# Attention and mixer on one core: where score steps stand between matmuls, and how the last output tile is stored

## The chip, the core and the metric

One NeuronCore of a Trainium2 chip runs the whole program. Its engines are TensorE (PE, matmuls; PEld is its weight load), VectorE (DVE), ScalarE (ACT), GpSimd (POOL) and SyncE (SP), which here only issues DMAs. Each engine executes its own queue in order; semaphores hold an instruction until what it reads is there and what it overwrites has been read. The metric is the time of one execution in microseconds on the device, the median of several runs.

## The reference

Eight items of 448 tokens, 12 heads of 64. Attention with normalised queries and keys, then a mixer on the result: a low-rank product over tokens, and a two-layer MLP.

```python
q_n, k_n = rmsnorm(q, g_q), rmsnorm(k, g_k)
attn = softmax(q_n @ k_n^T / sqrt(64))            # per item and head, 448 x 448
x = (attn @ v) as [8, 448, 768]                   # heads side by side
u = x + (x^T @ U @ V)^T                           # U: 448 x 32, V: 32 x 448
out = u + max(u @ w_ch1, 0) @ w_ch2               # 768 -> 3072 -> 768
```

## The kernel before

Work comes in two kinds, kept in two lists that are written out when the kernel is built. `att` holds attention steps, `mlp` holds mixer steps. A loop at the end takes from one or the other and so fixes the order of every engine's queue.

Attention goes by groups of four heads (24 groups, three an item; group 18, say, is heads 0 to 3 of item 6) and, inside, by pairs of heads (two a group, six an item). `load` brings q, k and v of a group; `squares` (ACT or POOL) and `sums` (VectorE, one reduction for q, one for k, L162) give the sums of squares; `scale_all` takes the roots on ACT (L169, L170) and scales q, k and v on POOL (L193 to L203). From group 6 on, `turn_dma` transposes q and k by DMA (issued by SP, L378 and L380) and `take_dma` multiplies the transposed queries by the gains on POOL (L386).

`Spair(b, pr)` computes all scores of one pair of heads: two matmuls into two banks `sl` (L427), four into `sc` (L436), one into a third bank `sl` (L438); ACT then takes five exponentials (L429, L439, L441). `V(b, pr, half)` is the product with the values (L462, L466), divided by the row sums on VectorE (L469, L470).

The mixer of item b: `mix_t(b)` (L485) is x^T U, cast by VectorE to `tb` (L487); `mix_tr(b)` (L492) transposes it, VectorE copies it to `tT` (L494); eight `mix_rows(b, w, half)` (L537) multiply with V and add to x on VectorE (L542), and after each second one SP issues the DMA transpose of u into `uT` (L548). 24 steps `up(b, ht)` (L554, six matmuls of 448 columns) make the hidden layer, with ReLU on ACT into `hT` (L561). `down(b, col, half, part, 4)` (L586) makes half an output tile of 128 tokens in four parts of six matmuls of 384 columns; behind the last part VectorE adds u (L596), and after the second half SP stores the tile, 64 x 768 numbers twice (L604).

Eight PSUM banks: four belong to `sc` (two tiles of two banks), four to the pool `ps`, from which `sl`, `pv`, `pu`, `pw`, `pm`, `ph` and `po` all come. Each new tile is given the bank of an earlier one, so its first matmul waits until whoever read that earlier tile last is done.

`due(c)` says how much attention (`ca`) should be placed when `c` of the mixer's cost is placed. An attention step is taken when it is due and `ready`. `at` holds, for PE, ACT and DVE, an estimated time up to which that engine has work, moved by `runs`; before the change `ready` looks at it only in the first part (`ca < a_one`), and refuses a `Spair` straight behind a mixing step. `mix_t`, `mix_tr` and `mix_rows` of the next item stand among the `down` steps of the current one; where one comes up right behind a `Spair`, a `down` part is drawn ahead of it (`after_pair`).

Of the kernel before, what the change touches and what calls it, by code (L numbers as in the profile page):

```python
# [9 lines left out]
FP32 = mybir.dt.float32  # L10
# [3 lines left out]
ALU = AluOpType  # L14
# [5 lines left out]
DMA_FROM = 6  # L20
# [6 lines left out]
def kernel(  # L27
# [13 lines left out]
    nc = tc.nc  # L41
    B, H, S, D = q.shape
    dm = H * D
# [3 lines left out]
    P = 128  # L47
    NT = S // 64
    NJ = S // P
    SM = NJ * P  # L50
    R = S - SM
# [6 lines left out]
    KH = dh // P  # L58
    NPAIR = H // 2
    HALF = dm // 2  # L60
# [9 lines left out]
    outp = ctx.enter_context(tc.tile_pool(name="outp", bufs=3))  # L70
    ps_sc = ctx.enter_context(tc.tile_pool(name="ps_sc", bufs=2, space=bass.MemoryType.PSUM))
    ps = ctx.enter_context(tc.tile_pool(name="ps", bufs=4, space=bass.MemoryType.PSUM))
# [199 lines left out]
    w2b = consts.tile([P, KH, dm], BF16)  # L272
    hT = consts.tile([P, KH, 512], BF16)
# [63 lines left out]
    at = {"pe": 0.0, "act": 0.0, "dve": 0.0}  # L337
    exp_done = {}

    def runs(eng, us):  # L340
        at[eng] = us + (at["pe"] if eng == "pe" else max(at["pe"], at[eng]))

    qk, es, xs = {}, {}, {}
# [136 lines left out]
    def mix_t(b):  # L480

        pt = ps.tile([P, KD, rank], FP32, name="pu", tag="ps")
        for dt in range(KD):
            for j in range(NW):
                nc.tensor.matmul(pt[:, dt, :], xs[b][:, j, dt * P:(dt + 1) * P], Ub[:, j if j < NJ else NJ + b % 2, :],  # L485
                                 start=(j == 0), stop=(j == NW - 1))
        nc.vector.tensor_copy(tb_bufs[b % 2][:, :KD * rank], pt.rearrange("p k r -> p (k r)"))  # L487

    def mix_tr(b):
        pt = ps.tile([P, 2, P], BF16, name="pw", tag="ps")  # L490
        for i in range(2):
            nc.tensor.transpose(pt[:, i, :], tb_bufs[b % 2][:, i * P:(i + 1) * P], ident)  # L492
        tTs[b] = headp.tile([P, 2, P], BF16, name="tT", tag="tT")
        nc.vector.tensor_copy(tTs[b], pt)  # L494

    def mix_t0(lo, hi, scalar=False):

        pt = ps.tile([P, 512], FP32, name="pu0", tag="ps")
        for j in range(NW):
            nc.tensor.matmul(pt[:, :hi - lo], Uz[:, j, :], xs[0][:, j, lo:hi], start=(j == 0), stop=(j == NW - 1))  # L500
        if scalar:
            nc.scalar.copy(tz[:, lo:hi], pt[:, :hi - lo])
        else:
            nc.vector.tensor_copy(tz[:, lo:hi], pt[:, :hi - lo])
# [70 lines left out]
            nc.scalar.activation(hT[:, ht, off:off + S], ph, AF.Relu)  # L575

    down_ps, down_sb = {}, {}

    def down(b, col, half, part, nparts):
        key = (b, col, half)  # L580
        if part == 0:
            down_ps[key] = ps.tile([P, HALF], FP32, name="po", tag="ps")
        po = down_ps[key]
        n = KH // nparts
        for ht in range(part * n, (part + 1) * n):
            nc.tensor.matmul(po, hT[:, ht, col:col + P], w2b[:, ht, half * HALF:(half + 1) * HALF],  # L586
                             start=(ht == 0), stop=(ht == KH - 1))
        runs("pe", 0.98)
        if part < nparts - 1:
            return  # L590
        runs("dve", 0.55)
        h = slice(half * HALF, (half + 1) * HALF)
        if half == 0 or b == 0:
            down_sb[(b, col)] = outp.tile([P, dm], FP32, name="ob", tag="ob")
        ob = down_sb[(b, col)]
        nc.vector.tensor_tensor(ob[:, h], po, urows(b, col, half), ALU.add)  # L596
        if half == 1 or b == 0:
            h = h if b == 0 else slice(0, dm)

            def rows(b, j):  # L600
                return out[b].rearrange("(p j) d -> j p d", j=NT)[j]
            for i in range(2):
                o = rows(b, i * NJ + col // P) if col != SM else rows(b - i, 2 * NJ)
                nc.sync.dma_start(o[:, h], ob[i * R:(i + 1) * R, h])  # L604
# [10 lines left out]
    def weights(n):  # L615
        for f, a in todo[:n]:
            f(*a)
        del todo[:n]
# [51 lines left out]
    for i, (b, pr) in enumerate(pairs):  # L670
        if b == 0:
            continue
        gi, a = divmod(i, 2)
# [78 lines left out]
    mlp = []  # L752
    for b in range(B):
        for ht in range(KH):
            mlp.append((0.38, up_part, (b, ht, 4, KD), b) if b == 0 and ht < 2 else (1.14, up, (b, ht), b))
            if b < ROWS_FROM and ht % 2 == 0 and ht < 4 * NW:
                mlp.append((0.17, mix_rows, (b, ht // 4, ht // 2 % 2), b))
        cols = (64, 192, 320) if b % 2 == 0 else (384, 0, 128, 256)
        n = len(cols) * 8
        nb = b + 1  # L760
        pre = {}
        if ROWS_FROM <= nb < B:
            pre[n - PRE[nb > 1]] = [(0.77, mix_t, (nb,), nb)]
            pre[n - PRE[nb > 1] + 1] = [(0.11, mix_tr, (nb,), nb)]
            for piece in range(2 * NW):
                pre.setdefault(n - PRE[nb > 1] + 2 + (piece if nb > 1 else piece // 2), []).append(
                    (0.17, mix_rows, (nb, *divmod(piece, 2)), nb))
        tiles = [(col, half) for col in cols for half in range(2)]
        if b == 0:
            tiles.sort(key=lambda t: t[1])  # L770
        for c, (col, half) in enumerate(tiles):
            for part in range(4):
                mlp.extend(pre.get(c * 4 + part, []))
                mlp.append((0.98, down, (b, col, half, part, 4), b))

    a_, b_ = PARTS
    squares_part(0, *a_)
# [40 lines left out]
    ca = cm = 0.0  # L818
    a_from = done_at[0]
    a_all = sum(c for c, _, _ in att[a_from:])  # L820
    a_one = sum(c for c, _, _ in att[a_from:done_at[1]])
# [9 lines left out]
    def due(c):  # L831

        if c < m_one:
            return min(a_one - 0.01, a_one * c / (m_one - 3.0))
        c -= m_one
        if c < REST:
            return a_one - 0.01
        if c < SECOND:
            return a_one + (a_two - a_one) * (c - REST) / (SECOND - REST)
        return a_two + (a_all - a_two) * (c - SECOND) / (m_end - m_one - SECOND)  # L840

    def mixes(f):
        return f in (mix_t, mix_tr, mix_rows)

    def ready(f, a):
        if f is Spair:
            return im == 0 or not mixes(mlp[im - 1][1])
        if ca >= a_one:
            return True
        if f is V:  # L850
            return exp_done[a[:2]] <= at["pe"] + 0.1
        return f is not Srows or at["act"] <= at["pe"] + 0.6

    later, turning, after_pair = [], False, False
    while ia < len(att) or im < len(mlp):
        if not turning:
            for f, a in later:
                f(*a)
            later.clear()
        if ia == a_from and im == 0:  # L860
            at.update(pe=0.0, act=0.0, dve=0.0)
        may_mlp = im < len(mlp) and ia >= done_at[mlp[im][3]]
        take_att = ia < len(att) and (not may_mlp or ca <= due(cm) and ready(*att[ia][1:]))
        if take_att:
            c, f, a = att[ia]
            if f is load:
                later.append((f, a))
            else:
                f(*a)
            after_pair = f is Spair or after_pair and f is not V  # L870
            if ia >= a_from:
                ca += c
            ia += 1
            if f is scale_all and a[0] < DMA_FROM:
                weights(2)
            if f is T and a == (DMA_FROM - 1, 1):
                nc.vector.memset(kp[:, 2 * NJ:], 0.0)
        else:
            if after_pair and mixes(mlp[im][1]):
                nb, n, moved = mlp[im][3], im, []  # L880
                while mixes(mlp[n][1]) and mlp[n][3] == nb:
                    e = next(i for i in range(n, len(mlp)) if mlp[i][1] is down)
                    moved += [mlp[e], *mlp[n:e]]
                    n = e + 1
                mlp[im:n] = moved
            after_pair = False
            c, f, a, _ = mlp[im]
            f(*a)
            turning = f is mix_t and a[0] > 0 or turning and a != (a[0], NW - 1, 1)
            cm += c  # L890
            im += 1
# [30 lines left out]
```

## Time and profile before

| | |
|---|---|
| median of 3 runs | 586.94 us (586.19 to 587.28) |
| the profiled execution, its own time | 586.64 us |
| its span in the profile | 584.8 us |
| granted TensorE clock | 0.999 |
| TensorE, busy share of the span | 98% |
| VectorE, ScalarE, GpSimd | 34%, 53%, 36% |

A row of the timeline reads: start in us, length in us, engine, line, operation, output<-inputs, shape, count, and in brackets the idle time before it with what ended it. A row of a group reads: busy time, mean ns of one, idle time before and what ended it. Rows of the chain of waits have start, length and what was waited for. Matmuls are pipelined: the next starts before the last one's modelled end, so lengths of PE rows overlap.

### The profile page before, as it was taken

Reading aid. Unit: us, or ns where it says so; the run is one execution under the profiler, and the core shown is the slowest. Engines: PE = TensorE matmul, PEld = TensorE weight load, DVE = VectorE, ACT = ScalarE, POOL = GpSimd, SP = SyncE. Lnnn points to the kernel's source line nnn. Section 1 sums busy time; section 2 is a strip of 40 time slices with the busy share of each in tenths; the row PEclk is TensorE's granted clock in tenths of the full one; section 3 lists DMA queues with packets and bytes.
Section 4 is the critical chain, followed back from the end, with each engine's and each line's share of the span. In section 5 each row is a group of like instructions: output and inputs, shape, how many; then the busy total and the mean of one; then the engine's idle time right before and its main releaser. Section 6 shows DMA issues by size and latency. Waiting matters only on the chain.

```text
span 584.8 us, 11725 instructions
## 1 busy us (share of the span) xinstructions
PE 572.2 (98%) x4826; PEld 338.2 (58%) x4826; DVE 196.8 (34%) x458; ACT 307.9 (53%) x510; POOL 210.3 (36%) x310
## 2 busy tenths in 40 slices
PE   8899999999999999999999999999999999999996
PEld 7555556555665555655556555665556655655563
DVE  6676656212352232521235231442034310410011
ACT  7866661677445776277653578457753344014200
POOL 5995684265314515334523433441531000000000
PEclk9999999999999999999999999999999999999999
DMA  8899999683546642585246735375204210420022
GB/s 229 170 241 241 244 233 231 119 220 52 133 78 167 153 106 35 139 212 130 36 122 109 180 104 123 66 172 149 35 25 92 48 28 1 68 61 1 1 54 55
DMA packets 104509, 68.21 MB, mean 117 GB/s; under 512 B 66568, under 2 KB 101256, under 8 KB 104456
## 3 DMA queue, kind: packets, MB, share of 16 engines
q1 hardware_dynamic: 95044, 58.03, 42.6%
q0 software_dynamic: 9408, 9.44, 9.6%
q8 instruction: 38, 0.62, 0.4%
q14 instruction: 15, 0.12, 0.1%
q10 hardware_dynamic: 4, 0.00, 0.0%
HBM read 52.20 MB, written 11.01 MB: 108 GB/s over the span
## 4 chain that ended last, share of the span: by engine, by line
PE 91%; DMA 3%; DVE 2%; POOL 1%; ACT 1%; issue 1%; SPq 1%; POOLq 0%; ACTq 0%
PE ph L554 36%; PE po L586 36%; PE pv L466 6%; PE sc L436 2%; PE sl L427 2%; PE sl L438 2%; PE pv L462 2%; PE pm L537 2%; DMA qf<-in_q_dram 1%; PE sc L415 1%; ACT E L416 1%; DMA vf<-in_v_dram 1%; DVE ssq L162 1%; DMA qT<-qn 1%; PE pu L485 1%
## 5 line engine op out<-in xcount | busy, mean ns | idle before, releaser
L586 PE MATMUL po<-w2b,hT 128*128 128x384 bf16 x1344 | 237.4, 326 | 0.0
L554 PE MATMUL ph<-uT,w1b 128*128 128x448 bf16 x1140 | 228.7, 352 | 0.0
L586 PEld LDWEIGHTS <-hT 128*128 128x128 bf16 x1344 | 126.8, 98 | 75.5 <-issue 0.6
L554 PEld LDWEIGHTS <-w1b 128*128 128x128 bf16 x1140 | 108.3, 98 | 93.8 <-issue 0.7
L561 ACT ACTIVATE hT<-ph 128x448 bf16<-128x448 f32 x184 | 98.0, 550 | 120.2 <-PE ph L554 118.9
L429 ACT ACTIVATE E<-sl,gg 128x448 bf16<-128x448 f32 x72 | 41.5, 629 | 75.9 <-PE sl L427 75.9
L386 POOL TENSOR_SCALAR qT<-qT,gg 128x448 bf16<-128x448 bf16 x36 | 50.5, 1402 | 81.6 <-DMA qT<-qn 65.2
L193 POOL TENSOR_TENSOR qn<-qf,rs 128x384 bf16<-128x384 f32 x36 | 29.9, 829 | 132.4 <-ACT rs L170 127.5
L469 DVE RECIPROCAL r<-pv 128x4 f32<-128x4 f32 x96 | 17.4, 182 | 167.8 <-PE pv L466 167.6
L441 ACT ACTIVATE E<-sc,gg 128x896 bf16<-128x896 f32 x72 | 69.0, 1022 | 0.0
L596 DVE TENSOR_TENSOR ob<-po,x 128x384 f32<-128x384 f32 x48 | 26.7, 557 | 103.8 <-PE po L586 103.4
L466 PE MATMUL pv<-va,E 128*128 128x65 bf16 x1152 | 57.1, 194 | 0.0
L466 PEld LDWEIGHTS <-E 128*128 128x128 bf16 x1152 | 50.5, 98 | 6.3
L162 DVE TENSOR_REDUCE ssq<-sq 128x14 f32<-128x896 f32 x45 | 46.8, 1078 | 2.4 <-ACT sq L140 2.3
L462 PE MATMUL pv<-vl,E 128*128 128x130 bf16 x192 | 42.2, 220 | 0.3 <-ACT E L416 0.2
L470 DVE TENSOR_TENSOR x<-pv,r 128x256 bf16<-128x256 f32 x96 | 40.7, 424 | 3.3
L416 ACT ACTIVATE E<-sc,gg 128x896 bf16<-128x896 f32 (+1 forms) x42 | 37.5, 950 | 4.1 <-PE sc L415 4.1
L542 DVE TENSOR_TENSOR x<-pm,x 128x384 bf16<-128x384 f32 x48 | 26.2, 552 | 16.5 <-PE pm L537 14.2
L193 POOL TENSOR_TENSOR kp<-kf,rs 128x384 bf16<-128x384 f32 x36 | 29.8, 828 | 0.0
L169 ACT ACTIVATE rs<-ssq,eps 128x28 f32<-128x28 f32 (+1 forms) x25 | 7.8, 314 | 33.4 <-DVE ssq L162 29.2
L462 PEld LDWEIGHTS <-E 128*128 128x128 bf16 x192 | 18.7, 97 | 9.7 <-issue 2.0
L439 ACT ACTIVATE E<-sl,gg 128x448 bf16<-128x448 f32 x36 | 22.9, 637 | 0.0
(102 smaller groups left out, 387.9 us busy)
## 6 DMA issues: line engine op xcount, KB each, us to landing
qf<-in_q_dram SPq DMA_DIRECT2D x23, 448.0 KB, 3.7
kf<-in_k_dram SPq DMA_DIRECT2D x23, 448.0 KB, 6.4
out_dram<-ob SPq DMA_DIRECT2D x50, 192.0 KB, 2.8
vf<-in_v_dram SPq DMA_DIRECT2D x48, 192.0 KB, 5.9
w1b<-in_moe_w_ch_dram POOLq DMA_DIRECT2D x4, 1152.0 KB, 19.8
w2b<-in_moe_w_ch_dram POOLq DMA_DIRECT2D x8, 576.0 KB, 17.7
vf<-in_v_dram SPq DMA_DIRECT2D x48, 32.0 KB, 5.7
out_dram<-ob SPq DMA_DIRECT2D x12, 96.0 KB, 3.6
```

The lines of the kernel that those rows point to most:

```text
L162: nc.vector.tensor_reduce(ssqs[gi][:, i, :], sqs.pop((gi, i)), AX, ALU.add)
L193: nc.gpsimd.tensor_tensor(main.rearrange("p (t i) d -> p i t d", i=2), src[:, c, :2 * NJ].rearrange("p (i t) d -> p i t d", i=2), rs[:, c, ...
L386: nc.gpsimd.tensor_scalar(qT[:, a], qT[:, a], gg[:, 0:1], None, ALU.mult)
L416: nc.scalar.activation(es[(b, pr)][:, 2 * r:2 * r + n, :], sc[:, :n, :S], AF.Exp, scale=scal, bias=bias)
L429: nc.scalar.activation(E[:, 4 + i, :], ts[i], AF.Exp, scale=scal, bias=bias)
L441: nc.scalar.activation(E[:, 2 * r:2 * r + 2, :], tiles[r][:, :, :S], AF.Exp, scale=scal, bias=bias)
L462: nc.tensor.matmul(pv[:, i].rearrange("p e d -> p (e d)"), E[:, 2 * NJ, w:w + P], vl[:, lp, :], start=True, stop=False)
L466: nc.tensor.matmul(pv[:, i, e, :], E[:, 2 * j + e, w:w + P], va[:, (first_h + step * e) * NJ + j, :], start=False, stop=(e == 1 and j == N ...
L470: nc.vector.tensor_tensor(xs[b].rearrange("p i (h d) -> p i h d", d=D)[:, 2 * half:2 * half + 2, h0:h0 + step + 1:step, :], pv[:, :, :, :D ...
L554: nc.tensor.matmul(ph, w1b[:, dt, ht * P:(ht + 1) * P], uT[:, dt, off:off + S], start=(dt == 0), stop=(dt == KD - 1))
L561: nc.scalar.activation(hT[:, ht, off:off + S], ph, AF.Relu)
L586: nc.tensor.matmul(po, hT[:, ht, col:col + P], w2b[:, ht, half * HALF:(half + 1) * HALF], start=(ht == 0), stop=(ht == KH - 1))
```

## The change

Three things.

1. The steps `mix_t` and `mix_tr` now move the estimates in `at`.
2. `ready` has new rules for all of the run: a `Spair` is taken only if VectorE's estimate is at most 0.3 us and ACT's at most 1.0 us past PE's; a `V` waits for one mixer step if a `Spair` or another `V` has been taken since the last one; `sums` of groups past 6 aren't taken within a few mixer steps of `mix_t` and `mix_tr`.
3. The last output tile (item 7, token columns from 256) is no longer two halves of four parts. `down_end` makes it in three accumulations of 384, 256 and 128 columns, 24 matmuls each; each is added and stored alone, 64 rows by SP and 64 rows by ACT's queue.

In the program that results, everything up to `down(0, 64, 1, 3)` stands as before. Behind it these steps stand elsewhere; all else keeps its order.

- Spair (2,0), (2,1), (5,4), (6,3), (7,2), (7,4), (7,5): behind one more `down` part; for (6,3) and (7,4) also behind one more `mix_rows`.
- Spair (2,2): behind `up(1, 3)`.
- Spair (3,2): behind three more `down` parts and `mix_rows(2, 3, 1)`.
- Spair (4,2): behind two more `down` parts and `mix_rows(3, 3, 0)` and `(3, 3, 1)`.
- Item 4's mixing: `mix_t(4)` and `mix_tr(4)` come before sums(17) and scale_all(17); Spair (5,2) five `down` parts later, behind `mix_tr(4)` and four `mix_rows(4)`; V(5, 1, 0) and V(5, 1, 1) behind it, turn_dma(17) with it.
- Item 5's mixing: the same for `mix_t(5)`, `mix_tr(5)`, sums(20), scale_all(20), Spair (6,2), V(6, 1), turn_dma(20).

On SP, the transposes of groups 17 and 20 stand one `uT` transpose later than before; on ACT one `hT` comes ahead of the exponentials of Spair (2,2), and the three stores of the last tile stand at the end.

```diff
         nc.vector.tensor_copy(tb_bufs[b % 2][:, :KD * rank], pt.rearrange("p k r -> p (k r)"))
+        runs("pe", 0.62)
+        runs("dve", 0.35)
...
         nc.vector.tensor_copy(tTs[b], pt)
+        runs("pe", 0.11)
+        runs("dve", 0.3)
...
+    ENDS = (HALF, 5 * P, dm)
+
+    def down_end(b, col, piece):
+        lo, hi = (0, HALF) if piece == 0 else ENDS[piece - 1:piece + 1]
+        if piece == 0:
+            down_sb[(b, col)] = outp.tile([P, dm], FP32, name="ob", tag="ob")
+        ob = down_sb[(b, col)]
+        po = ps.tile([P, HALF], FP32, name="po", tag="ps")[:, :hi - lo]
+        for ht in range(KH):
+            nc.tensor.matmul(po, hT[:, ht, col:col + P], w2b[:, ht, lo:hi], start=(ht == 0), stop=(ht == KH - 1))
+        nc.vector.tensor_tensor(ob[:, lo:hi], po, xs[b][:, col // P, lo:hi], ALU.add)
+        for i, eng in enumerate((nc.sync, nc.scalar)):
+            eng.dma_start(out[b].rearrange("(p j) d -> j p d", j=NT)[i * NJ + col // P][:, lo:hi],
+                          ob[i * R:(i + 1) * R, lo:hi])
...
+        if b == B - 1:
+            tiles = tiles[:-2]
...
+    mlp.extend((3.9 * w, down_end, (B - 1, cols[-1], piece), B - 1) for piece, w in enumerate((1.0, 0.67, 0.34)))
...
     def ready(f, a):
         if f is Spair:
-            return im == 0 or not mixes(mlp[im - 1][1])
+            if im > 0 and mixes(mlp[im - 1][1]):
+                return False
+            return at["dve"] <= at["pe"] + 0.3 and at["act"] <= at["pe"] + 1.0
+        if f is V and ca >= a_one and (after_pair or after_v):
+            return False
+        if f is sums and a[0] > DMA_FROM:
+            return not any(m[1] in (mix_t, mix_tr) for m in mlp[max(0, im - 1):im + 3])
         if ca >= a_one:
             return True
...
-            after_pair = f is Spair or after_pair and f is not V
+            after_pair = after_pair or f is Spair
+            after_v = after_v or f is V
...
-            after_pair = False
+            after_pair = after_v = False
```

More of the change, by code (lines that the diff above doesn't have):

```diff
@@ L852, in ready @@
         return f is not Srows or at["act"] <= at["pe"] + 0.6
-    later, turning, after_pair = [], False, False
+    later, turning, after_pair, after_v = [], False, False, False
     while ia < len(att) or im < len(mlp):
```

## The prediction

> **What bounds the kernel now.** I read the page first, then the chain of waits, then the timeline of TensorE at every place the change touches, and last the end of the span.
>
> ```profile
> span 584.8 us, 11725 instructions
> ...
> PE 572.2 (98%) x4826; PEld 338.2 (58%) x4826; DVE 196.8 (34%) x458; ACT 307.9 (53%) x510; POOL 210.3 (36%) x310
> ...
> PE 91%; DMA 3%; DVE 2%; POOL 1%; ACT 1%; issue 1%; SPq 1%; POOLq 0%; ACTq 0%
> ```
>
> TensorE carries 91% of the chain, so the kernel ends when its queue has run dry. A busy share of 98% hides short waits, though, because the modelled ends of pipelined matmuls cover them. Waits have to be read from starts: how long after its first matmul a step gets to its last. For a pair of heads (`Spair`) I measure from its first L427 to its L438. From 476.66 us on nothing is left to win inside the stream, as the chain shows:
>
> ```profile
> 476.66 19.30 PE ph L554 x102
> ...
> 499.85 0.59 PE pu L485 x24
> ...
> 501.43 0.11 PE pw L492 x2
> ...
> 502.51 0.17 PE pm L537 x3
> ...
> 548.64 31.21 PE po L586 x192
> ...
> 579.88 0.56 DVE ob L596
> ```
>
> Here every piece starts where the one before it ends; after 579.85 TensorE is idle while the last tile is added, stored and landed: 4.96 us to the end of the span. One matmul of 384 columns costs 31.21/192 = 0.163 us, a `down` part of six 0.98; `mix_t` costs 0.59, `mix_tr` 0.11, a `mix_rows` 0.17.
>
> **Where TensorE waits today, and what the change does there.** Timeline of TensorE at the four `Spair` that are late:
>
> ```profile
> 112.78 1.87 PE L554 MATMUL ph<-uT,w1b 128*128 128x448 bf16 x9
> 115.72 0.37 PE L427 MATMUL sl<-qT,kT 64*128 64x448 bf16 x2 [1.08 <-POOL qT L386]
> ...
> 116.40 0.36 PE L438 MATMUL sl<-qT,kT 128*128 128x448 bf16 x1
> ...
> 173.72 1.14 PE L586 MATMUL po<-w2b,hT 128*128 128x384 bf16 x6
> 174.79 0.36 PE L427 MATMUL sl<-qT,kT 64*128 64x448 bf16 x1
> 175.67 0.35 PE L427 MATMUL sl<-qT,kT 64*128 64x448 bf16 x1 [0.52 <-DVE x L542]
> ...
> 176.40 0.35 PE L438 MATMUL sl<-qT,kT 128*128 128x448 bf16 x1
> ...
> 238.96 0.71 PE L427 MATMUL sl<-qT,kT 64*128 64x448 bf16 x2
> ...
> 239.98 0.36 PE L438 MATMUL sl<-qT,kT 128*128 128x448 bf16 x1
> ...
> 302.59 0.36 PE L427 MATMUL sl<-qT,kT 64*128 64x448 bf16 x2
> ...
> 303.98 0.35 PE L438 MATMUL sl<-qT,kT 128*128 128x448 bf16 x1 [0.65 <-DVE tb L487]
> ```
>
> Undisturbed, L427 to L438 takes 116.40 - 115.72 = 0.68 us. At 174.79 it takes 1.61, at 238.96 1.02, at 302.59 1.39: waits of 0.93, 0.34 and 0.71 us. At 115.72 the wait is ahead of the first matmul. The nine matmuls from 112.78 span 1.87 us, of which the last lasts 0.35, so they are 0.19 apart and the next could start at 114.48, plus the 0.10 that always stands ahead of a pair (six matmuls of 0.163 from 173.72 end at 174.69, the pair starts at 174.79): 114.58. Wait: 1.14 us. Together 3.12 us.
>
> The causes, from VectorE's timeline and the chain:
>
> ```profile
> 173.08 2.07 DVE L162 TENSOR_REDUCE ssq<-sq 128x14 f32<-128x896 f32 x2
> 175.07 0.55 DVE L542 TENSOR_TENSOR x<-pm,x 128x384 bf16<-128x384 f32 x1
> ...
> 238.73 0.54 DVE L596 TENSOR_TENSOR ob<-po,x 128x384 f32<-128x384 f32 x1
> ...
> 301.60 2.07 DVE L162 TENSOR_REDUCE ssq<-sq 128x14 f32<-128x896 f32 x2
> 303.58 0.35 DVE L487 CAST tb<-pu 128x192 bf16<-128x192 f32 x1
> 305.45 0.29 DVE L494 COPY tT<-pw 128x256 bf16<-128x256 bf16 x1 [1.53 <-PE pw L492]
> ```
>
> ```profile
> 109.76 4.32 DMA qT<-qn
> ...
> 114.27 1.41 POOL qT L386
> ```
>
> Three of the waits are one thing: the two reductions of `sums` hold VectorE for 2.07 us, the adds and copies behind them free PSUM banks late, and the pair wants three banks of `ps`. The fourth is the transposed queries, ready at 115.68.
>
> **Spair(2,2), at 115.72.** It moves behind one more `up` of 6 x 0.19 = 1.13 us, so TensorE arrives at 115.71, and qT is ready at 115.68 if the queries' chain keeps its time. It does: its first link, the transposes at 109.76, is issued by SP in an order that is unchanged up to there, and (2,0) and (2,1), each one `down` later, leave the stores ahead of it where they were. Gain 1.14. The margin is 0.03 us, so up to some tenths may stay. ACT now has one `hT` more ahead of the five exponentials and the three `up` behind the pair follow at once. That pattern stands in the trace, behind Spair(2,4):
>
> ```profile
> 139.80 0.22 PE L462 MATMUL pv<-vl,E 128*128 128x130 bf16 x1
> ...
> 140.48 1.29 PE L554 MATMUL ph<-uT,w1b 128*128 128x448 bf16 x6
> 141.61 0.22 PE L462 MATMUL pv<-vl,E 128*128 128x130 bf16 x1
> ...
> 142.11 1.11 PE L554 MATMUL ph<-uT,w1b 128*128 128x448 bf16 x5
> ```
>
> A `V` takes 0.50 at 141.61 and 0.68 at 139.80, where the next `up` waits for a bank that a late `hT` frees. I charge 0.19 for the same at V(2,1,0); bounds 0 and 0.5. Net gain 0.95.
>
> **Spair(3,2), at 174.79.** It moves behind three `down` parts and a `mix_rows`, 3 x 0.98 + 0.17 = 3.1 us. The banks it takes are then those of the last two mixing adds, which follow the one at 175.07 at 0.56 each: free 1.4 and 2.0 us after the old start. Gain 0.93.
>
> **Spair(4,2), at 238.96.** Two parts and two `mix_rows` later, 2.3 us. The adds that it then needs end 0.8, 1.4 and, for the third bank, which it wants 0.7 into the pair, 2.1 us after the old start. Gain 0.34.
>
> **Spair(5,2), at 302.59.** Here the new order differs most: `mix_t` and `mix_tr` of item 4 now precede sums(17), and the pair comes five `down` parts later. Counted from the start of `mix_t`: tb is cast by 1.2, `mix_tr` runs at 1.6, tT ends by 2.2, the sums hold VectorE until 4.3, and behind them queue the adds of two `mix_rows` (4.8, 5.3), the `down` add (5.9) and two more `mix_rows` (6.4, 7.0). TensorE wants the first of these banks at 5.1, for a `down`, and the pair starts at 7.3, wanting banks free at 5.9 and 6.4 and, at 8.0, the one free at 7.0. Nothing waits; the least margin is 0.3 us. Gain 0.71; bounds 0.71 and, if the sums start 1 us late, nothing.
>
> **Spair(6,2), with sums(20), scale_all(20) and V(6,1) moved likewise.** Nothing waits there today, so it can only lose; by the same count its least margin is 0.3. Cost 0, upper bound 0.7 (what (5,2) waits now). Moved with it are the root on ACT, the scaling on POOL and turn_dma(20), turn_dma(17) alike on SP, now behind a second uT transpose. The room for queries to be late, at the tightest group behind the first wait (14), from POOL's and TensorE's timelines:
>
> ```profile
> 254.23 1.40 POOL L386 TENSOR_SCALAR qT<-qT,gg 128x448 bf16<-128x448 bf16 x1 [9.59 <-DMA qT<-qn]
> ```
>
> ```profile
> 259.94 0.36 PE L427 MATMUL sl<-qT,kT 64*128 64x448 bf16 x2
> ```
>
> Ready at 255.63, wanted at 259.94: 4.3 us, and TensorE will be 2.2 us early by then even if nothing on the queries' way moves with it. turn_dma(17) and (20) newly wait only for that transpose and the add at 7.0 of the count above, ahead of the pair at 7.3. Cost 0.
>
> **The other moved pairs**, (2,0), (2,1), (5,4), (6,3), (7,2), (7,4), (7,5), go one part later and wait for nothing today. Several now stand one part behind the end of a `down` tile and take the bank of that tile: it is free some 0.2 us after its last matmul plus the add of 0.56, and wanted after a part of 0.98 and the 0.10: 0.3 us to spare. Cost 0. Their exponentials come a microsecond later on ACT, but the products V of a pair stand behind the next pair, so nobody waits for them.
>
> Middle: -0.95 - 0.93 - 0.34 - 0.71 = -2.93 us; bounds -3.3 and -1.9.
>
> **The end.** Rows:
>
> ```profile
> L604 SPq DMA_DIRECT2D out_dram<-ob x62: 466/562/1565, 85.9 to 581.0; - x62
> ...
> DMA to landing us min/median/max: 2.1/2.9/6.0
> ```
>
> ```profile
> 580.47 1.11 SPq L604 DMA_DIRECT2D out_dram<-ob  x2
> ```
>
> ```profile
> L504 DVE CAST x<-pu 128x128 bf16<-128x128 f32 x2 | 0.6, 285 | 0.0
> ```
>
> ```profile
> 9.47 0.94 PE L240 MATMUL busy<-ident 128*128 128x128 bf16 x14
> ```
>
> TensorE: pieces of 384, 256 and 128 columns instead of two of 384. No row has 256; 128 columns cost (0.94 - 0.22)/13 = 0.056 (0.22 being the length of a single one, as at 139.80), 384 cost 0.163, and both are 0.43 ns a column, so 0.109: 24 x (0.163 + 0.109 + 0.056) = 7.87 against 7.82, +0.05. Last add: 128 columns, 0.29 by the cast of that width, against 0.56: -0.27. The second store's issue goes to ACT's queue, idle by then: the second was issued at 581.0, the first at 580.47: -0.53; if ACT's issue took the 1.57 us of the longest SP row it would be +0.6 instead. Landing: 32 KB, not 192: between nothing and 2.9 - 2.1 = 0.8; I take 0.5. Sum -1.25; bounds -1.7 and +0.4.
>
> The Trainium skill speaks against the narrow piece: "TensorE: Matmul & The Clock Gate", Back-to-back issue gap, puts a stream of weight loads and 128-column matmuls at about 81 ns each. By that estimate the last piece costs 24 x 25 ns = 0.6 us more and the end gains 0.65. The row's 56 ns, with a load ahead of every matmul, speaks for the lower price.
>
> On the landing, "DMA: Bandwidth & Descriptors", Anatomy of one DMA, gives for the GpSimd path a fixed 2.0 us plus bytes at 436 GB/s. By that estimate the smaller store saves 0.38, not 0.5, and the end gains 1.1; the row's minimum of 2.1 fits the fixed part.
>
> **Sum.** -2.93 - 1.25 = -4.2 us. The profiled execution took 586.64, 1.84 over its span and 0.30 under the median of the three runs; so 582.4 for an execution like it, 582.7 on the median. I say 582.6.
>
> **The rivals.** *The waits move but stay.* VectorE's reductions are as long as before and the estimates in `at` are not the chip's clock; the 3 us come back at `mix_rows` or `down`, and the end alone gains: 585.5. For it: margins of 0.03 and 0.3 us. Against: the reckoning above at each place. 0.11.
>
> *The end gains nothing*, because a store on ACT is slow to issue or the last landing is as late as today: 583.8. 0.10.
>
> *The narrow matmuls wait for their weights.* Every matmul loads new ones:
>
> ```profile
> L586 PEld LDWEIGHTS <-hT 128*128 128x128 bf16 x1344 | 126.8, 98 | 75.5 <-issue 0.6
> ```
>
> Were a load the bound, the last piece would take 24 x 0.098 = 2.35 us instead of 1.34: 583.6. Against: the 0.056 above, also with a load each. 0.04. The 81 ns of the Trainium skill's page on TensorE, quoted above, would make it 583.2.
>
> *The moved pairs wait, and it is slower.* Place: the eight pairs that are moved without need, (6,2) among them, each of which now follows a `down` add or mixing adds on VectorE by some 0.3 us. If VectorE is later than that, each waits. At the 0.34 us of (4,2) that is 2.7 us, and 585.3; at the 0.93 of (3,2) it is 7.4, and 590.0. It decides from 4.3/8 = 0.54 us each, which needs VectorE 0.8 us late at all eight. For it: 0.3 us is little beside one reduction. Against: only at (6,2) do reductions stand just ahead, and there they are counted. 0.05.
>
> The forecast itself has 0.70: 581.3 to 584.2, the bounds of both parts not all on one side, and 0.4 for the scatter of runs. With the second and third rival inside and half of the first left out, 581.3 to 585.0 holds eight in ten. No change means within 0.2%, 1.2 us, about what a measurement of this kernel can tell apart. Faster 0.89, same 0.06 (half the first rival), slower 0.05.
>
> **What would show it.** Right: L427 to L438 at 0.68 us at all four places, no idle time charged to POOL's qT ahead of (2,2), V(2,1,0) at 0.68; last matmul some 2.9 us earlier; from the last add to the end of the span about 3.7 us instead of 4.96. Wrong: a `down` or `mix_rows` near 300 or 363 us that starts late behind VectorE; a POOL qT row that ends after TensorE has come; a DMA issue on ACT of over 1 us.

## The result, and the profile after

The changed kernel takes 582.44 us (median of 6 runs, 581.59 to 584.02), the kernel before 586.57 (6 runs, 585.24 to 587.85): a ratio of 0.9922, 95% interval 0.9903 to 0.994. The forecast was 582.6, with 581.3 to 585.0 as its range. The profiled execution took 582.16, its span 580.3 against 584.8.

The page of the changed kernel, first lines and the shares of the chain:

```profile
span 580.3 us, 11778 instructions
...
PE 570.9 (98%) x4850; PEld 338.7 (58%) x4850; DVE 196.3 (34%) x459; ACT 308.2 (53%) x510; POOL 210.2 (36%) x310
...
PE 92%; ACT 2%; DMA 1%; POOL 1%; DVE 1%; issue 1%; SPq 0%; POOLq 0%; ACTq 0%
```

TensorE is still 98% busy. As before, the gain can't be seen in the shares; it is in the starts. TensorE's timeline at the four pairs that waited (in the changed kernel `up` is L558, `down` L605):

```profile
110.94 4.70 PE L558 MATMUL ph<-uT,w1b 128*128 128x448 bf16 x24
115.79 0.36 PE L427 MATMUL sl<-qT,kT 64*128 64x448 bf16 x2
...
116.46 0.36 PE L438 MATMUL sl<-qT,kT 128*128 128x448 bf16 x1
...
176.81 0.36 PE L427 MATMUL sl<-qT,kT 64*128 64x448 bf16 x2
...
177.49 0.36 PE L438 MATMUL sl<-qT,kT 128*128 128x448 bf16 x1
...
239.25 0.36 PE L427 MATMUL sl<-qT,kT 64*128 64x448 bf16 x2
...
239.93 0.36 PE L438 MATMUL sl<-qT,kT 128*128 128x448 bf16 x1
...
305.91 0.36 PE L427 MATMUL sl<-qT,kT 64*128 64x448 bf16 x2
...
306.58 0.36 PE L438 MATMUL sl<-qT,kT 128*128 128x448 bf16 x1
```

From L427 to L438 it is 0.67 or 0.68 us at all four; before it was 1.61, 1.02 and 1.39 at the last three. Ahead of the first a wait is left: 24 matmuls 0.19 apart from 110.94 end at 115.48, with the usual 0.10 the pair could start at 115.58, and it starts at 115.79: some 0.2 us instead of 1.14.

The end, from the timeline (the last tile's matmuls are L592, its adds L593, its stores L595) and from the list of DMA issues in the view of the DMA queues:

```profile
568.84 8.02 PE L592 MATMUL po<-w2b,hT 128*128 128x384 bf16 x72
...
573.52 4.16 SPq L595 DMA_DIRECT2D out_dram<-ob  x3
573.53 4.19 ACTq L595 DMA_DIRECT2D out_dram<-ob  x3
...
576.90 0.29 DVE L593 TENSOR_TENSOR ob<-po,x 128x128 f32<-128x128 f32 x1 [0.92 <-PE po L592]
```

```profile
out_dram<-ob ACTq DMA_DIRECT2D x1, 32.0 KB, 2.0
```

The last add starts at 576.90 and the span ends at 580.28: 3.38 us, 4.96 before. In the trace's events the last two issues start together at 577.22 (0.47 us on SP, 0.50 on ACT) and land at 578.99 and 579.25.

The account of the 4.56 us between the spans: waits at (2,2), (3,2), (4,2), (5,2) 0.93 + 0.93 + 0.34 + 0.71 = 2.91; the mixer began 0.15 us earlier in this execution, which is no merit of the change; the end 1.58, less 0.06 that the narrower pieces cost TensorE. That makes 4.58.

### The profile page after: what moved, and what is told of

Same layout as the page of the kernel before. It is cut to its first block, busy times and chain, and to the rows that moved or that the text cites. A ratio compares the mean times of both kernels' runs of the same rounds, so it can differ in the third digit from the quotient of the medians.

```text
span 580.3 us, 11778 instructions
## 1 busy us (share of the span) xinstructions
PE 570.9 (98%) x4850; PEld 338.7 (58%) x4850; DVE 196.3 (34%) x459; ACT 308.2 (53%) x510; POOL 210.2 (36%) x310
## 4 chain that ended last, share of the span: by engine, by line
PE 92%; ACT 2%; DMA 1%; POOL 1%; DVE 1%; issue 1%; SPq 0%; POOLq 0%; ACTq 0%
PE ph L558 36%; PE po L605 36%; PE pv L466 6%; PE sc L436 2%; PE pv L462 2%; PE sl L427 2%; PE sl L438 2%; PE pm L541 2%; PE po L592 1%; ACT E L416 1%; PE sc L415 1%; DMA qT<-qn 1%; PE pu L485 1%; DMA qf<-in_q_dram 1%; PE pt L354 1%
## 5 line engine op out<-in xcount | busy, mean ns | idle before, releaser
L605 PE MATMUL po<-w2b,hT 128*128 128x384 bf16 x1296 | 229.6, 326 | 0.0
L558 PE MATMUL ph<-uT,w1b 128*128 128x448 bf16 x1140 | 228.7, 352 | 0.0
L605 PEld LDWEIGHTS <-hT 128*128 128x128 bf16 x1296 | 122.1, 98 | 71.8
L558 PEld LDWEIGHTS <-w1b 128*128 128x128 bf16 x1140 | 108.3, 98 | 93.7 <-issue 0.7
L429 ACT ACTIVATE E<-sl,gg 128x448 bf16<-128x448 f32 x72 | 41.6, 630 | 71.7 <-PE sl L427 71.7
```

The costliest lines, as they stand in the source:

```text
L429: nc.scalar.activation(E[:, 4 + i, :], ts[i], AF.Exp, scale=scal, bias=bias)
L558: nc.tensor.matmul(ph, w1b[:, dt, ht * P:(ht + 1) * P], uT[:, dt, off:off + S], start=(dt == 0), stop=(dt == KD - 1))
```

## The experiments

Each kernel is a small edit of the one before or of the changed one. Where no interval is given, a kernel was run once, and what is read from it is read from its profile.

**The two halves of the change apart.** `order_only` is the changed kernel with the old last tile:

```diff
-        if b == B - 1:
-            tiles = tiles[:-2]
...
-    mlp.extend((3.9 * w, down_end, (B - 1, cols[-1], piece), B - 1) for piece, w in enumerate((1.0, 0.67, 0.34)))
```

> The changed order with the old last tile (two halves of four parts, one store of the whole tile by SP). Theory (four local waits and, apart from them, the end): the span falls by 2.9 us against the kernel before, to about 581.9, and the stretch from the last add to the end of the span stays at 4.96. Time about 583.7 where the kernel before takes 586.6, ratio 0.995. Rival (the new tail carries more than its share, because the waits of the middle come back elsewhere): under 1.5 us gained. At Spair(2,2) 0.2 us of waiting for the queries stays, as in the changed kernel.

`tail_only` is the changed kernel with the old rules, the new tile kept:

```diff
-            if im > 0 and mixes(mlp[im - 1][1]):
-                return False
-            return at["dve"] <= at["pe"] + 0.3 and at["act"] <= at["pe"] + 1.0
-        if f is V and ca >= a_one and (after_pair or after_v):
-            return False
-        if f is sums and a[0] > DMA_FROM:
-            return not any(m[1] in (mix_t, mix_tr) for m in mlp[max(0, im - 1):im + 3])
+            return im == 0 or not mixes(mlp[im - 1][1])
```

> The old order with the new last tile. Theory: TensorE's last matmul starts where it did (within 0.1 us), the stretch from the last add's start to the end of the span falls from 4.96 to 3.4 us, the span by 1.6 us to about 583.3, the time to about 585.0, ratio 0.997. All four waits of the old order stay: L427 to L438 of Spair(3,2), (4,2), (5,2) at 1.6, 1.0 and 1.4 us, and 1.1 us ahead of (2,2). Rival (order and tail do not add up, since the order also changes what is in flight at the end): less than 1 us or more than 2.2.

Measured: `order_only` 583.98 us, 0.9942 of the kernel before (0.992 to 0.9963), span 582.3. `tail_only` 585.23, 0.9968 (0.995 to 0.9986), span 583.1. The kernel before had 586.77 there. By the medians the order brings 2.8 us and the end 1.5, 4.3 together, where the whole change brought 4.1 (and 3.3 in the repeat further below). The intervals of the two ratios reach a microsecond and more either way, so that the two halves add is shown no closer than that. In the profile of `tail_only` the three later waits stand as before, 0.93, 0.34 and 0.71 us, and the end is 3.40 us. In `order_only` the three are gone and the end is the old one, 4.96 us from the last add to the end of its span of 582.33:

```profile
577.37 0.56 DVE L615 TENSOR_TENSOR ob<-po,x 128x384 f32<-128x384 f32 x1 [3.34 <-PE po L605]
```

Its span is 0.4 longer than expected: 0.87 us of wait is left ahead of Spair(2,2), where the changed kernel's first profile had 0.2, and its mixer began 0.25 earlier than in the kernel before. The order of the work there is the same in both. That is taken up below.

**Are the reductions the cause?** `short_sums` is the kernel before, whose `sums` from group 7 on reduce 8 of the 64 squares (the scale of the root is adjusted); it leaves out most of the sums of squares:

```diff
-        nc.vector.tensor_reduce(ssqs[gi][:, i, :], sqs.pop((gi, i)), AX, ALU.add)
+        sq = sqs.pop((gi, i))
+        n = 8 if gi > DMA_FROM else D
+        nc.vector.tensor_reduce(ssqs[gi][:, i, :], sq[:, :, :n], AX, ALU.add)
```

> The kernel before, with the reductions of sums from group 7 on over 8 of the 64 squares of each head and token only (the norms are then estimated from an eighth of the numbers). Order and everything else unchanged. Theory (the reductions' 2.07 us on VectorE hold the PSUM banks): with some 0.4 us instead, L427 to L438 is 0.7 us at Spair(3,2), (4,2) and (5,2) in the old order, while the 1.1 us ahead of (2,2), which wait for the queries, stay. Span 2.0 us lower, about 582.9. Rival (the pair stands too close behind the mixing adds, whatever the reductions take): over 0.3 us of waiting stays at two of the three.

Measured: 583.67 us, span 581.9. All three waits are gone, with the old order. VectorE's and TensorE's timelines (the edit shifts lines by two: the pair is L429 to L440 here):

```profile
299.31 0.43 DVE L164 TENSOR_REDUCE ssq<-sq 128x14 f32<-128x112 f32 x2
299.67 0.35 DVE L489 CAST tb<-pu 128x192 bf16<-128x192 f32 x1
```

```profile
300.31 0.36 PE L429 MATMUL sl<-qT,kT 64*128 64x448 bf16 x2
...
300.98 0.36 PE L440 MATMUL sl<-qT,kT 128*128 128x448 bf16 x1
```

At (5,2) 0.67 us, and likewise at 173.78 and 237.03. That the two reductions of 2.07 us made those waits is shown. The span fell 1 us more than expected: the wait ahead of (2,2) is gone too, since the queries landed early in this execution (below). Whether the edit has a part in that is not shown.

**One rule at a time.** `gate_only` is the kernel before with the new condition for pairs and the two moved estimates, without the rules for V and sums; `sums_only` has the rule for sums alone.

```diff
         if f is Spair:
-            return im == 0 or not mixes(mlp[im - 1][1])
+            if im > 0 and mixes(mlp[im - 1][1]):
+                return False
+            return at["dve"] <= at["pe"] + 0.3 and at["act"] <= at["pe"] + 1.0
```

> Of the change only the new condition for pairs of heads and the estimates of mix_t and mix_tr; sums(17) and sums(20) stay ahead of the mixing, V is placed as before, old last tile. Theory (VectorE's reductions are the cause, the pair's place only decides who meets them): the waits at (2,2), (3,2) and (4,2) go, all but 0.2 us, and that at (5,2) goes from the pair but turns up at mix_tr(4), which now comes 1 us after mix_t(4) and needs the cast tb that stands behind the 2 us of sums(17): some 1.4 us there. Span about 0.9 + 0.93 + 0.34 + 0.71 - 1.4 = 1.5 us below that of the kernel before, about 583.4. Rival (placing the pairs by the estimates is what helps, the rule for sums adds nothing): no wait at mix_tr, span 581.9.

```diff
             return im == 0 or not mixes(mlp[im - 1][1])
+        if f is sums and a[0] > DMA_FROM:
+            return not any(m[1] in (mix_t, mix_tr) for m in mlp[max(0, im - 1):im + 3])
```

> The kernel before with the rule for sums alone: no reductions in the step ahead of a mix_t or mix_tr or within two behind, from group 7 on; the condition for pairs and the end as before. Theory: the wait at (5,2) (0.71 us) is gone, since tb and tT are then copied ahead of the reductions; those at (3,2) (0.93) and (4,2) (0.34) are changed only where their sums move. Span 584.1 if the wait at (2,2) is that of the first profile. Rival: the reductions only come later in front of the adds, and the wait turns up at a mix_rows or at the pair behind.

`gate_only`: 585.29 us, span 583.5, where the kernel before had 586.77. The pairs (3,2), (4,2) and (5,2) no longer wait (at (2,2) 0.65 us is left), but the reductions, still ahead of the cast of `tb`, now hold up `mix_tr(4)`. Its TensorE and VectorE timelines:

```profile
299.38 1.14 PE L605 MATMUL po<-w2b,hT 128*128 128x384 bf16 x6
301.85 0.29 PE L494 MATMUL pw<-ident,tb 128*128 128x128 bf16 x2 [1.33 <-DVE tb L487]
```

```profile
299.46 2.07 DVE L162 TENSOR_REDUCE ssq<-sq 128x14 f32<-128x896 f32 x2
301.44 0.35 DVE L487 CAST tb<-pu 128x192 bf16<-128x192 f32 x1
```

A `down` part takes 0.98, so the transposes could start at 300.36: 1.49 us of wait in place of the old 0.71.

`sums_only`: 587.80 us, span 586.0, where the kernel before had 586.97: no gain. Of the 1.2 us by which its span is longer than that of the kernel before, 0.55 is a longer wait at (2,2) in this one execution. (3,2) and (4,2) wait as before. At (5,2) the rival came true, with another engine than it named:

```profile
304.62 0.36 PE L438 MATMUL sl<-qT,kT 128*128 128x448 bf16 x1
304.82 1.14 PE L605 MATMUL po<-w2b,hT 128*128 128x384 bf16 x6
306.60 0.33 PE L541 MATMUL pm<-tT,Vm 128*128 128x128 bf16 x3 [0.64 <-ACT E L429]
```

The pair itself does not wait, but the `mix_rows` one part behind it does, 0.80 us (306.60 less 304.82 and 0.98), for a bank that the pair's exponentials on ACT free late; the same at (6,2), where nothing had waited. Neither rule gains anything at (5,2) alone. In the changed kernel the sums go behind the copies and the pair behind the mixing steps, and nothing waits; the rule for V is in it too, and its part is not separated.

**What sets the wait ahead of Spair(2,2)?** The changed kernel unaltered, once more:

> The changed kernel once more, unaltered, to see what of its remaining wait ahead of Spair(2,2) differs from one execution to the next. Theory: this wait is set by the queue of DMA issues on SP and by the landing of the transposes, not by TensorE, so the wait is another one (0.1 to 0.9 us) although the order of the work is the same; the other three pairs again take 0.68 us from L427 to L438. Rival: the 0.22 us of the first profile are a fixed property of the order and come out again within 0.05. Time 582.5, ratio 0.992.

Measured: 583.04 us (581.60 to 584.33), 0.9946 (0.9929 to 0.9964), span 581.9. The queue of DMA issues on SP in the changed kernel's first profile, with POOL's scaling of the queries:

```profile
101.38 4.44 SPq L552 DMA_TRANSPOSE uT<-x  x3
105.91 1.21 SPq L552 DMA_TRANSPOSE uT<-u_rest  x1
107.21 2.46 SPq L623 DMA_DIRECT2D out_dram<-ob  x4
109.78 1.21 SPq L378 DMA_TRANSPOSE qT<-qn  x1
...
114.33 1.40 POOL L386 TENSOR_SCALAR qT<-qT,gg 128x448 bf16<-128x448 bf16 x1 [10.10 <-DMA qT<-qn]
```

and in the second, with TensorE's `up` steps and the pair:

```profile
104.17 3.92 SPq L552 DMA_TRANSPOSE uT<-x  x3
108.19 1.21 SPq L552 DMA_TRANSPOSE uT<-u_rest  x1
109.49 2.52 SPq L623 DMA_DIRECT2D out_dram<-ob  x4
...
111.76 4.70 PE L558 MATMUL ph<-uT,w1b 128*128 128x448 bf16 x24
...
112.11 2.48 SPq L378 DMA_TRANSPOSE qT<-qn  x1
...
117.37 0.36 PE L427 MATMUL sl<-qT,kT 64*128 64x448 bf16 x2 [0.91 <-DMA kT<-kp]
```

The same instructions in the same order; the whole train is 2.3 to 2.8 us later in the second, while TensorE is 0.82 later (111.76 against 110.94). The wait is 0.98. The profile charges it to the transposed keys (`kT`, L380), whose transpose stands behind that of the queries on SP: they landed 0.03 us after POOL had scaled the queries. In `gate_only`, `sums_only` and `tail_one_queue` it is the same by 0.03 to 0.06, so there the queries and the keys hold the pair together. SP stands idle ahead of the first uT transpose, and the view of SP's waits from 95 to 118 us says for what: the loads of v that it issued before. First profile, then second:

```profile
SPq L552 <- DMA vf<-in_v_dram: 0.8, 2, 0.6
```

```profile
SPq L552 <- DMA vf<-in_v_dram: 1.7, 1, 1.7
```

The start of that first uT transpose against the start of `up(1, 0)` falls into two groups over all profiles of this study, 9.4 to 9.7 us ahead of it (early) or 7.2 to 7.9 us (late). SP's longest wait for v in that window is 0.5 to 0.6 us in the seven early profiles, 1.7 to 2.0 in the seven late ones. Both groups occur in both orders, one late profile of four with the pair in its old place and six of ten with it moved; whether the order has a part in it is not shown. Eleven of them:

| profile | uT issue | qT issue | TensorE comes | pair starts | wait |
|---|---|---|---|---|---|
| old place: before | 101.36 | 109.76 | 114.57 | 115.72 | 1.15 |
| tail_only | 101.08 | 109.54 | 114.22 | 115.45 | 1.23 |
| short_sums | 101.82 | 110.13 | 114.72 | 114.72 | 0 |
| sums_only (late) | 102.92 | 110.92 | 114.27 | 115.97 | 1.70 |
| new place: the first profile | 101.38 | 109.78 | 115.57 | 115.79 | 0.22 |
| tail_two | 101.99 | 110.30 | 115.99 | 115.99 | 0 |
| order_only (late) | 102.88 | 110.76 | 115.46 | 116.33 | 0.87 |
| gate_only (late) | 102.99 | 110.86 | 115.34 | 115.98 | 0.65 |
| after_again (late) | 104.17 | 112.11 | 116.39 | 117.37 | 0.98 |
| tail_one_queue (late) | 104.17 | 112.04 | 116.04 | 117.19 | 1.15 |
| tail_64 (late) | 103.24 | 111.12 | 115.66 | 116.86 | 1.20 |

(TensorE comes: start of the last matmul of the `up` ahead, plus 0.19 and 0.10.) With the loads landing late the new place still waits 0.65 to 1.20 us, so what is left behind one `up` is between nothing and as much as the kernel before waited. In `short_sums` the queries were at POOL 2.7 us after their issue (110.13 to 112.82), in the kernel before 4.5 (109.76 to 114.27): the transposes' own landing differs as well.

In the profiles of three further kernels this wait is gone. `later22` puts the pair one `up` further, `later22_two` two:

```diff
             if im > 0 and mixes(mlp[im - 1][1]):
                 return False
+            if a == (2, 2) and mlp[im][1] is up and mlp[im][2] < (1, 5):   # (1, 6) in later22_two
+                return False
```

> The changed kernel with Spair(2,2) behind one more up (1.13 us). Theory: TensorE comes to the pair at about 116.7 us, the queries of group 7 are scaled by 115.4 to 116.3, so the wait of 0.2 to 0.9 us ahead of the pair is gone and nothing else changes: 582.0, ratio about 0.991. Rival: the exponentials of the pair now come later on ACT, and the V behind it or an up waits 0.2 us for its bank: no gain over the changed kernel.

> The changed kernel with Spair(2,2) behind two more up (2.27 us), as the candidate that beats both kernels. In the seven profiles of the new order the pair could start between 0.0 and 1.2 us after TensorE came to it; behind one more up (1.13 us) it did not wait in one profile, behind two it cannot wait in any of them. Theory: 582.0, ratio about 0.9915, no wait ahead of the pair. Rival: only one up is left between the pair and the products of pair (2,1), so the exponentials hold up an hT on ACT and the next up or V waits 0.2 to 0.5 us for a bank: 582.4, no better than one up.

`stores_pool` clears SP's queue instead:

```diff
-                nc.sync.dma_start(o[:, h], ob[i * R:(i + 1) * R, h])
+                eng = nc.gpsimd if b == 0 and half == 1 and col in (64, 192) else nc.sync
+                eng.dma_start(o[:, h], ob[i * R:(i + 1) * R, h])
```

> The changed kernel with the four stores that stand on SP just ahead of the queries' transposes of group 7 (those of the output tiles of item 0 at columns 64 and 192) issued by POOL, which has no work between 104 and 114 us. Theory: the wait ahead of Spair(2,2) comes from SP's queue, where loads of v, transposes of uT, these stores and then the transposes follow each other; without the stores (2.46 us of issue) the transposes start 2.4 us sooner, the queries are ready by 113.3 to 114.8 us, before TensorE comes at 115.6, and the wait is gone in every execution: 582.0 and less scatter, ratio about 0.991. Rival: the transposes are held by something else (the scaling on POOL, the landing of other transfers) and start or land no sooner: 582.5. Against it also: an issue on POOL may take longer than on SP's 0.55 us.

Its queues, POOL's and SP's, and the pair:

```profile
102.81 3.92 SPq L552 DMA_TRANSPOSE uT<-x  x3
...
104.46 2.32 POOL L624 DMA_DIRECT2D out_dram<-ob  x4
...
106.82 1.23 SPq L552 DMA_TRANSPOSE uT<-u_rest  x1
108.16 1.20 SPq L378 DMA_TRANSPOSE qT<-qn  x1
...
111.88 1.40 POOL L386 TENSOR_SCALAR qT<-qT,gg 128x448 bf16<-128x448 bf16 x1 [5.10 <-DMA qT<-qn]
...
115.31 0.36 PE L427 MATMUL sl<-qT,kT 64*128 64x448 bf16 x2
```

The loads landed late here too (102.81), yet the transposes follow uT at once and the queries are scaled by 113.28, 2.0 us before the pair, which starts without a wait. So SP's queue is the path to (2,2), which was the theory. In time it is 582.87 us (581.92 to 583.76), 0.9934 (0.9918 to 0.995), no better than the changed kernel. In its profile `up(1, 0)` starts 0.15 late, behind the last transpose of `uT`, which landed at 110.54: with the stores on POOL beside them the `uT` transposes took 3.7 to 4.1 us from issue to landing, 2.4 to 2.6 in the changed kernel's first profile. What else the runs without a profile hold is not known.

`later22`: 582.20 us (581.85 to 584.72), 0.994 (0.9922 to 0.9957), against 583.04 for the changed kernel run beside it; `later22_two`: 582.50 (581.99 to 583.12), 0.9926 (0.9907 to 0.9944), and its pair, two `up` on, has no wait either:

```profile
111.49 6.97 PE L558 MATMUL ph<-uT,w1b 128*128 128x448 bf16 x36
118.40 0.36 PE L427 MATMUL sl<-qT,kT 64*128 64x448 bf16 x2
```

Nor did anything new wait behind it, against its rival. Both profiles belong to the early group, though, so no profile shows these two with the loads landing late; that one `up` more would then nearly do (1.13 us against waits of 0.65 to 1.20) and two would do is worked out from the table. The twelve runs of the changed kernel have a median of 582.55 and reach from 581.59 to 584.33; the six of `later22_two` lie within 1.13 us. That one of the three is faster than the changed kernel is not shown: the intervals overlap by far.

**The end.** `tail_one_queue` issues all stores of the last tile on SP, `tail_two` makes that tile in two halves, `tail_64` in 384, 320 and 64 columns:

```diff
-        for i, eng in enumerate((nc.sync, nc.scalar)):
+        for i, eng in enumerate((nc.sync, nc.sync)):      # tail_one_queue
-    ENDS = (HALF, 5 * P, dm)
+    ENDS = (HALF, dm)                                     # tail_two, with two steps for three
+    ENDS = (HALF, 11 * P // 2, dm)                        # tail_64
```

> The changed kernel with all six stores of the last tile issued by SP, none by ACT. Theory: the end's gain comes in part from the second issue no longer standing behind the first: the last store is issued one SP issue (0.47 us) later, and lands and ends that much later: from the last add's start to the end of the span 3.9 us instead of 3.4, span 0.5 longer than the changed kernel's but for what the queries' wait at (2,2) makes of it. Rival: the landing sets the end and takes the later issue up: no change.

> The changed kernel with the last tile in two accumulations of 384 columns, each stored alone over both queues. Theory: against three pieces the last add takes 0.27 us longer (0.56 for 0.29) and the last stores carry 98 KB each instead of 33, 0.25 us more to land by a line between the 2.03 us of 33 KB and the 2.65 of 197 KB: 3.9 us from the last add's start to the end of the span instead of 3.4; between the kernel before (4.96) and the changed one. Rival: the bytes count for nothing and the two queues for all: 3.66.

> The changed kernel with the last tile in 384, 320 and 64 columns instead of 384, 256 and 128. Theory with no floor under a matmul: the last piece of 24 takes 24 x 0.028 = 0.67 us, the whole tile as long as before the edit, the last add 0.2 instead of 0.29, the landing 0.05 sooner: the end 0.15 us sooner. Rival: the weights' loads set a floor of about 0.055 us under a matmul: the last piece stays at 1.3 us, and the last matmul comes 0.6 us later, the end 0.45 later.

Their times were 583.88, 582.98 and 583.36 us with spans of 582.07, 581.16 and 581.49, but the wait at (2,2) differs among them by up to 1.2 us (the table), so only the stretch from the last add counts. The last adds of the three:

```profile
578.30 0.29 DVE L593 TENSOR_TENSOR ob<-po,x 128x128 f32<-128x128 f32 x1 [0.91 <-PE po L592]
```

```profile
577.03 0.56 DVE L593 TENSOR_TENSOR ob<-po,x 128x384 f32<-128x384 f32 x1 [3.34 <-PE po L592]
```

```profile
577.96 0.23 DVE L593 TENSOR_TENSOR ob<-po,x 128x64 f32<-128x64 f32 x1 [0.21 <-PE po L592]
```

To the end of the span it is 3.77 us in `tail_one_queue`, 0.39 more than in the changed kernel: the second queue is worth that, a little less than the 0.5 expected, since a store landed 1.89 us after its issue on SP and 2.03 on ACT. The Trainium skill's page "DMA: Bandwidth & Descriptors", Rules for kernel authors, says that spreading DMAs over issuing engines adds no bandwidth and only saves issue time; the trace agrees, the 0.39 being of the size of one issue (0.47).

In `tail_two` it is 4.13, 0.23 over the theory and well over its rival: the add 0.27 longer, the landing 2.38 instead of 2.03 (96 KB for 32), and 0.13 more from the landing to the end.

In `tail_64` it is 3.53, longer than with 128 columns although the add is shorter, where the theory had the end 0.15 sooner: the add is done at 578.18, but the issues of the piece before end only at 578.24 on SP and 578.28 on ACT, so the last one on ACT starts 0.19 us behind the add, 0.03 in the changed kernel. From there it lands after 2.07 us, though half as large, against 2.03. The narrow matmuls cost TensorE nothing. All matmuls of the last tile, in the changed kernel and in `tail_64`, first and last start at the end of each row:

```profile
L592 PE MATMUL po<-w2b,hT x72: 219/272/326, 568.8 to 576.6; 128*128 128x384 bf16 x24, 128*128 128x256 bf16 x24, 128*128 128x128 bf16 x24
```

```profile
L592 PE MATMUL po<-w2b,hT x72: 192/299/327, 569.9 to 577.7; 128*128 128x384 bf16 x24, 128*128 128x320 bf16 x24, 128*128 128x64 bf16 x24
```

Both tiles take 7.8 us. 24 x (0.163 + 0.136) = 7.2 of the second go to its wider pieces, which leaves 0.6 / 24, under 0.03 us, for a matmul of 64 columns, a new weight load with every one. With a floor of 0.055 the tile would take 0.7 more: the rival is out.

## Why the prediction was right

The mechanisms came out at three of the four waits and at the end; at the fourth the reasoning failed, and that the total still fits so closely is partly luck, since other terms made up for it.

- **(3,2), (4,2), (5,2): 0.93, 0.34, 0.71.** As forecast, to 0.01, and nothing waits at the eight pairs moved without need, (6,2) among them. The reductions as cause are shown by `short_sums`. The count along VectorE's queue for (5,2) came out too; counted from the start of `mix_t` at 298.58, VectorE's timeline has

```profile
300.68 2.07 DVE L162 TENSOR_REDUCE ssq<-sq 128x14 f32<-128x896 f32 x2
...
305.04 0.56 DVE L546 TENSOR_TENSOR x<-pm,x 128x384 bf16<-128x384 f32 x1 [0.29 <-PE pm L541]
```

  with the reductions done at 4.2 (forecast 4.3) and the last mixing add at 7.0 (7.0), and the pair starts at 7.3 (7.3). In `gate_only` such a count put 1.4 us at mix_tr(4), and 1.49 came. The 0.80 of `sums_only` is outside these counts: there ACT's exponentials hold the bank.
- **(2,2): 1.14, of which 0.19 was to be lost at V(2,1,0).** The step that failed is "its first link, the transposes at 109.76, is issued by SP in an order that is unchanged up to there". The order is unchanged, the time isn't: across the new place's seven profiles the transposes are issued from 109.78 to 112.11, and the wait left is 0 to 1.20, 0.7 in the mean. "Up to some tenths may stay" was too small a bound. What the move is worth depends on when the loads land: in the early group the wait is 1.15 and 1.23 in the old place (0 in short_sums, which is put aside here) and 0.22 and 0 in the new, about the 1.14 forecast; in the late group 1.70 in the one profile of the old place and 0.97 in the mean of five in the new, some 0.7. That the first profile is an early one was luck. V(2,1,0) did not wait: TensorE's timeline has

```profile
120.07 0.22 PE L462 MATMUL pv<-vl,E 128*128 128x130 bf16 x1
...
120.56 1.30 PE L558 MATMUL ph<-uT,w1b 128*128 128x448 bf16 x6
```

  0.49 us, so the 0.19 was charged for nothing, and in the profiled execution the two errors (0.22 left, 0.19 not lost) nearly cancel: middle 2.91 by waits, forecast 2.93.
- **The end: 1.25 forecast, 1.52 measured** (1.58 from the last add on, less 0.06 on TensorE). Add 0.27 as forecast. Second issue 0.52 for 0.53; by `tail_one_queue` the second queue alone is worth 0.39. Landing 2.65 to 2.03 = 0.62 for 0.5, which the prediction took from between two bounds: mis-sized by 0.12. From the landing to the end of the span 1.21 to 1.03: 0.18 that the sum had no term for. The narrow pieces cost TensorE 0.06 for 0.05.
- **The two prices of the Trainium skill.** The 81 ns that the Trainium skill's page "TensorE: Matmul & The Clock Gate", Back-to-back issue gap, gives would have made the last piece 0.6 us longer; 128 columns ran at 0.056 us, as the row of before said, and 64 at under 0.03. For the landing, the 0.38 worked out from the Trainium skill's "DMA: Bandwidth & Descriptors", Anatomy of one DMA, a fit for the GpSimd path, is too small for these stores by SP and ACT, 0.62 measured; its fixed 2.0 us is about what the 32 KB store took (2.03).
- **The rivals.** Waits that move: true at (5,2) for either of the rules for pairs and sums alone, false for the whole change. An end that gains nothing: out, by `tail_only`. Narrow matmuls that wait for weights: out, by `tail_64`. Moved pairs that wait: not seen.

Open is what makes the loads of v land early or late, and how the scatter of the runs without a profile (581.6 to 584.3) divides between that and the start of the program: in the two profiles of the changed kernel, 1.6 us apart in span, `up(1, 0)` starts 0.82 us apart and the wait at (2,2) differs by 0.76, which is all of it. The rule for V was not tried alone, nor the other two without it.

## What to carry to other kernels

A wait on a queue behind a long instruction is removed by counting that queue's work in order, from the long instruction to the last reader that matters; moving only the waiter or only the long instruction moves the wait (1.49 and 0.80 us for 0.71 here). A wait on a DMA is not fixed by an order: before a margin of 0.03 us is called a gain, look how far the time of that issue moves from one execution to the next, and which landings the issuing queue itself waits for. At the end of a program, make the last piece's add, issue and landing short and give it a second issuing queue, but not so small that the piece before it is still being issued.

## What the runs showed of the hardware

- Matmuls with a new weight load each ran at 0.163, 0.109, 0.056 and under 0.03 us for 384, 256, 128 and 64 columns: no floor shows down to 64.
- A store's landing counted from the start of its issue: 2.65 us for 192 KB, 2.38 for 96 KB (ACT), 2.03 for 32 KB (ACT), 1.77 for 32 KB issued at the same moment by SP.
- SP's issue of a DMA transpose took 1.2 us at the least and up to 2.5; four store issues by POOL took 2.32 us, by SP 2.46.
- The `uT` transposes landed 2.4 to 2.6 us after the start of their issue in the changed kernel, 3.7 to 4.1 in `stores_pool`, with four stores of POOL's in flight beside them.
